# A transformer block on one core: the same instructions in another written-out order of the five engines

## The chip, the core and the metric

The kernel runs on one core of a Trainium2 chip. The metric is the device time of one execution in microseconds (us), and a kernel's time is the median of its runs. The engines are named as in the profile: PE is the matrix engine (PEld its loading of weights), DVE the vector engine, ACT the scalar engine, POOL the GpSimd engine, SP the sync engine, which here only issues DMAs.

## What is computed

A pre-norm block of two parts on 2048 tokens of width 512, in bf16. Part A is linear attention with 32 heads of 16; part B is a gated MLP whose gate mixes the tokens with a 2048x2048 matrix.

```python
h   = x + A(layernorm(x), wqkv, wo)
out = h + B(layernorm(h), w_in, w_sp, b_sp, w_out)

def A(x, wqkv, wo):                 # S = 2048, D = 512, 32 heads
    q, k, v = split(x @ wqkv)
    phi = lambda t: where(t > 0, t + 1, exp(t)) + 1e-6
    kv  = einsum('bhsd,bhse->bhde', phi(k), v)
    den = einsum('bhqd,bhd->bhq', phi(q), sum_s phi(k)) + 1e-6
    o   = einsum('bhqd,bhde->bhqe', phi(q), kv) / den
    return o @ wo

def B(x, w_in, w_sp, b_sp, w_out):  # F = 1792, Fh = 896
    z  = gelu(x @ w_in)
    z1, z2 = z[..., :Fh], layernorm(z[..., Fh:])
    g  = einsum('ts,bsf->btf', w_sp, z2) + b_sp[:, None]
    return (z1 * g) @ w_out
```

## The kernel before

**Stages.** Tokens go in 16 tiles of 128. In the order of the span:

- 0 to 48 us, `k_unit` and `q_unit`: tiles of x are loaded and normalised (`stats` L535, then `rstd` L541 and L543 on POOL or Ln and Exp on ACT, then `norm` L580 on DVE). The first six tiles are transposed on PE (`pe_transposes`, L594, with a copy by ACT), the others by a DMA. Then come k = xn wqkv (L427), phi on ACT and DVE (L606 to L611), and the product of pk with xn over all tokens (L684).
- 48 to 75: v is folded into a matrix m; the denominators are products of pqT with zc (L801), their reciprocals are spread over partitions by DMAs (`spread`, L792), and DVE multiplies pqT by them (L817, "pqT<-pqT,r"). Then for each tile n, PE multiplies pqT by m, DVE adds x and sums the row in one instruction (L829, "h<-psum,x"), and ACT takes the squares ("sh<-h"). POOL turns the two sums into mean and reciprocal deviation: `moments` (L559, L561, L562) and `rpow` (L575) for tiles 0 and 1, `moments_pair` (L567 to L571) for the others. DVE normalises (L580, "hn<-h,st,rs"), and a DMA transposes hn into hnT (L460).
- 70 to 141: B's first matrix, as sums and seven products in place of eight (`hn_sums`, `cell3`, `cell2`). `add_on` (L866) adds a partial result within PSUM on DVE, and PE goes on in the same bank. gelu runs on ACT ("z<-psum", "z1t<-psum"). For z2, even tiles have their squares on ACT ("sq<-z") and `moments` and `rpow` on POOL; the others have bn_stats and bn_aggr on DVE (L943, L944) and L541 and L543 on POOL. `norm` (L580, "z<-z,st,rs") follows on DVE. `t1_sums` and `t_sums` (L863) make sums of z2.
- 104 to 216, overlapping: `mix` multiplies by w_sp, in sums and products again, partly nested twice (`nested`, products of 128x224, with copies within PSUM by ACT and additions by DVE, L1039). `gate` (L999) and `gate_p` (L1007, L1008) form z1*(g + b) on DVE; a DMA on SP transposes it ("zgT<-z1t"). The memory of z1t of some tiles is used again, so that gelu of a later tile waits for such a transpose.
- 143 to the end: `mo_pair` multiplies zgT by w_out (L1158 and L1170 on DVE add h), `mo` (L1138) does the last two tiles, and SP and ACT store.

**What sets the order.** The program first collects 1306 operations with their dependencies (`add`). `schedule` then reads one list of operation numbers from the string ORDER (L16); each engine runs its operations in the order in which they stand in that list. `emit` writes each engine's stream and a semaphore wait for each dependency on another engine or on a DMA that is not already covered. Every engine works through its queue in that order: an instruction that waits holds all that stand behind it on its engine.

```python
ids = np.frombuffer(zlib.decompress(base64.b85decode(ORDER)), np.uint16).tolist()
...
self.seq = [self.ops[i] for i in ids]
self.order = {e: [o for o in self.seq if o.eng == e] for e in self.ENGS}
```

The costs and latencies that the operations carry (`dve_cost`, `act_cost`, `lat=`) give start times in `schedule`; in this program these only sort the waits of one operation.

Of the kernel before, what the change touches and what calls it, by code (L numbers as in the profile page):

```python
# [252 lines left out]
def bass_sequential_preLN__linear_attn_block__mixer_gmlp__prompt_kernel(  # L253
# [155 lines left out]
    def bank(b, n=512, lo=0):  # L409
        return psum[:, b, lo:lo + n]  # L410
# [39 lines left out]
    def dve(fn, reads, writes, n, ps=False, acc=1, **k):  # L450
        return g.add("DVE", fn, reads, writes, cost=dve_cost(n, ps, acc), lat=95, **k)
# [63 lines left out]
    load_x("ACT", 1, 1, 2300)  # L515
    x2 = load_x("SP", 2, 1, 2300)
    load_x("ACT", 3, 1, 2550)
    first_load("SP", wqkv[:, 0:2, D:2 * D], A_wqkv[0:2 * P, D:2 * D], "wka", 4200)
    wk = first_load("ACT", wqkv[:, 2:4, D:2 * D], A_wqkv[2 * P:4 * P, D:2 * D], "wkb", 4400)
    for n, lat, behind in ((4, 4600, None), (6, 3400, x2), (8, 3850, wk), (10, 4000, wk), (12, 4200, wk), (14, 4400, wk)):  # L520
# [12 lines left out]
    def stats(src, k, n):  # L533
        s = st[k][:, n, :]
        dve(lambda v: v.bn_stats(s[:, 0:6], src[:, n, :]), [src[:, n, :]], [s[:, 0:6]], D)  # L535
        return dve(lambda v: v.bn_aggr(s[:, 6:8], s[:, 0:6]), [s[:, 0:6]], [s[:, 6:8]], 14)

    def rstd(s, r, n, w, col, neg, sign=1.0):

# [16 lines left out]
    def moments(s, col, n):  # L556

        mean, ve = s[:, col:col + 1], s[:, col + 1:col + 2]
        pool(lambda p: p.tensor_scalar(s[:, 2:3], s[:, 0:1], s[:, 0:1], -1.0 / (n * n), op0=ALU.mult, op1=ALU.mult), [s[:, 0:1]],  # L559
             [s[:, 2:3]], 240)  # L560
        pool(lambda p: p.tensor_scalar(ve, s[:, 2:3], s[:, 1:2], EPS_LN, op0=ALU.add, op1=ALU.add), [s[:, 1:3]], [ve], 240)  # L561
        pool(lambda p: p.tensor_scalar(mean, s[:, 0:1], 1.0 / n, None, op0=ALU.mult), [s[:, 0:1]], [mean], 190)  # L562

    def moments_pair(i, n):
        s, r = st[1][:, i:i + 2, :], rs[1][:, i:i + 2, 0:1]
# [6 lines left out]
             740)  # L572

    def rpow(ve, r):
        pool(lambda p: p.tensor_tensor(r, ve, expo[:, 0:1], ALU.pow), [ve, expo], [r], 620)  # L575
# [25 lines left out]
    def phi(dst, b, w=2, split=False):  # L601

        e, t = e_t[ecnt[0] % NE][:, 0:w, :], psum[:, b:b + w, :]
        ecnt[0] += 1
        act_exp(e, t, ACT.Exp, w * GW)
        dve(lambda v: v.tensor_scalar(e, e, 1.0, EPS_PHI, op0=ALU.min, op1=ALU.add), [e], [e], w * GW, acc=4)  # L606
        if split:
            act(dst, t, ACT.Identity, w * GW, bias=epst[:, 2:3], extra=[epst[:, 2:3]])
            dve(lambda v: v.tensor_tensor(dst, dst, e, ALU.max), [dst, e], [dst], w * GW, acc=2)
        else:  # L610
            dve(lambda v: v.scalar_tensor_tensor(dst, t, 1.0 + EPS_PHI, e, op0=ALU.add, op1=ALU.max),  # L611
                [t, e], [dst], w * GW, ps=True)

    def warmup(n, ns, behind=None):
        def fn(pe):
# [172 lines left out]
    def spread(tg, c, w):  # L788
        i = tg % 2
        src, dst = rcp[32 * c:32 * (c + 1), i:i + w, :], r16[tg // 2][:, c, i:i + w, :]  # L790
        src_ap = bass.AP(src.tensor, src.offset, [list(src.ap[0]), [0, 4], [1, w * GW]])
        g.add("SP", lambda q: q.dma_start(dst, src_ap), [rcp[:, i:i + w, :]], [dst], cost=700, lat=2200, dma=f"r{tg}{c // 2}").soft.add(win_last.i)  # L792

    for tg in range(NG):
        tok = slice(tg * GW, (tg + 1) * GW)
# [29 lines left out]
    for n in range(NT):  # L825
        b = AB[n % 3]
        matmuls(bank(b), [(pqT[:, c, n * P:(n + 1) * P], m[:, c, :]) for c in range(KD)])
        s = st[1][:, n, :]
        dve(lambda v, n=n, b=b, s=s: v.scalar_tensor_tensor(h[:, n, :], bank(b), 1.0, x[:, n, :], op0=ALU.mult, op1=ALU.add,  # L829
                                                            accum_out=s[:, 0:1]),  # L830
            [bank(b), x[:, n, :]], [h[:, n, :], s[:, 0:1]], D + 70, ps=True)
        act(sh_t[n % 2], h[:, n, :], ACT.Square, D, scale=D ** -0.5, accum=s[:, 1:2])
        if n < HPAIR:
            moments(s, 6, D)
            rpow(s[:, 7:8], rs[1][:, n, 0:1])
            done = [n]
        else:
            done = [n - 1, n] if n % 2 else []
            if done:
                moments_pair(n - 1, D)  # L840
        for i in done:
            hn = hn_t[i % NH]
            norm(HN(i), hn, h[:, i, :], st[1], rs[1], i, 6, D)
            g.last = dma_t(hnT[:, :, i * P:(i + 1) * P], hn, f"ht{i}")
# [8 lines left out]
    def half(b):  # L853
        return bank(b, HW)
# [76 lines left out]
    def z2_done(n, b):  # L931
# [7 lines left out]
        else:  # L939
            gl = act(dst, two(b), ACT.Gelu_apprx_tanh, FH)  # L940
            for k in (0, 1):
                c = slice(k * HW, (k + 1) * HW)
                dve(lambda v, c=c, k=k: v.bn_stats(s[:, 6 * k:6 * k + 6], z2[:, n, c]), [z2[:, n, c]], [s[:, 6 * k:6 * k + 6]], HW)  # L943
            dve(lambda v: v.bn_aggr(s[:, 12:14], s[:, 0:12]), [s[:, 0:12]], [s[:, 12:14]], 14)  # L944
# [23 lines left out]
    SETS = (0, 3)  # L968
    Z1C = {1: (0,), 3: (1,), 5: (4,), 7: (5,)}
    ZLATE = (2, 6, 3, 7)  # L970
    NEST, ONPOOL = (0, 3, 15, 7), ()
    HB = 2
    SQ = range(0, NT - 2, 2)
    w_sums(win2, wq1[1])
# [5 lines left out]
    for j in range(HT):  # L980
# [9 lines left out]
        for q in Z1C.get(j, ()):  # L990
# [3 lines left out]
            for n in (2 * q, 2 * q + 1):  # L994
                z1_tile(n, 6)

    def gate(n, c, b):
# [4 lines left out]
    cnt = [0]  # L1002

    def gate_p(n, c, b, p):
        o, u = z1[n][:, c], u_t[cnt[0] % 2]
# [225 lines left out]
```

## Time and profile before

| | us |
|---|---|
| median of 3 runs | 227.09 (226.91 to 227.54) |
| profiled execution, whole time | 227.38 |
| profiled execution, span | 225.5 |
| PE busy, share of the span | 218.1, 97% |
| DVE busy | 204.9, 91% |
| ACT busy | 138.0, 61% |
| POOL busy | 51.5, 23% |

The span runs from the first to the last instruction of the profiled execution; its whole time is 1.9 us longer. A line of the profile names the line of the kernel, the engine, the operation and `out<-in`; L12 is line 12 of the kernel, and a helper's line stands for all who call it (L427 is every product, L446 every ACT operation). In the timeline a line begins with start and duration in us; in square brackets stands how long the engine was idle before it, and who released it. Neighbouring instructions of one kind are shown as one line, with their number behind the x.

### The profile page before, as it was taken

What the parts mean: (1) busy time and instruction counts of PE and PEld (TensorE: products, weight loads), DVE (VectorE), ACT (ScalarE), POOL (GpSimd) and SP (SyncE); (2) the same over time, 40 slices, a digit from 0 to 9 for tenths busy, and PEclk for the clock granted to TensorE, in tenths of its full rate; (3) what the DMA queues carried; (4) which work ended last, traced back from release to release, by engine and by line L of the source; (5) the groups of instructions that cost most, each with busy time, mean ns of one, the idle gap of its engine ahead of it and who ended that gap; (6) DMA issues with size and microseconds to landing.
All of it is one profiled execution on the core that took longest, in us unless ns stands there. A gap on an engine that the chain in (4) does not pass through costs nothing.

```text
span 225.5 us, 3882 instructions
## 1 busy us (share of the span) xinstructions
PE 218.1 (97%) x1361; PEld 125.6 (56%) x1361; DVE 204.9 (91%) x473; ACT 138.0 (61%) x274; POOL 51.5 (23%) x134
## 2 busy tenths in 40 slices
PE   8899999999999999999999999999999999999995
PEld 7434444453334454544555555767678668885653
DVE  4899855699999999989999999999999999999884
ACT  5686735479969999999675335543235824664111
POOL 2455400000384874597720000000000000000000
PEclk9999999999999999999999999999999999999999
DMA  5736478936553344699990225999061520262474
GB/s 160 241 104 150 75 209 246 241 70 159 125 116 70 70 93 74 132 174 184 217 199 7 41 44 103 182 181 132 0 128 34 97 58 9 65 67 87 85 188 148
DMA packets 73907, 26.87 MB, mean 119 GB/s; under 512 B 63648, under 2 KB 73888, under 8 KB 73888
## 3 DMA queue, kind: packets, MB, share of 16 engines
q1 hardware_dynamic: 73184, 26.03, 54.8%
q10 hardware_dynamic: 704, 0.59, 0.9%
q8 instruction: 11, 0.18, 0.3%
q14 instruction: 8, 0.07, 0.1%
HBM read 6.95 MB, written 2.10 MB: 40 GB/s over the span
## 4 chain that ended last, share of the span: by engine, by line
PE 66%; ACT 13%; DVE 8%; POOL 5%; DMA 4%; issue 2%; SPq 1%; ACTq 0%
PE psum L427 59%; PE psum L684 6%; ACT z L446 3%; DMA x<-in_A_x_dram 3%; DVE h L829 2%; ACT z1t L446 2%; ACT sq L446 2%; POOL rs L575 2%; DMA zgT<-z1t 1%; DVE st L535 1%; ACT psum L446 1%; ACT p5z L446 1%; DVE h L1170 1%; ACT sh L446 1%; ACT ct L446 1%
## 5 line engine op out<-in xcount | busy, mean ns | idle before, releaser
L446 ACT ACTIVATE psum<-psum 128x448 f32<-128x448 f32 (+2 forms) x76 | 31.5, 425 | 36.6 <-PE psum L427 29.7
L427 PE MATMUL psum<-z,wt 128*128 128x448 bf16 (+1 forms) x216 | 41.9, 335 | 0.0
L427 PEld LDWEIGHTS psum<-z,wt 128*128 128x128 bf16 x216 | 21.1, 98 | 14.9
L427 PE MATMUL psum<-win,hnT 128*128 128x448 bf16 x112 | 26.3, 353 | 0.0
L446 ACT ACTIVATE e<-psum 128x1024 bf16<-128x1024 f32 (+1 forms) x18 | 16.7, 928 | 14.1 <-PE psum L427 13.6
L446 ACT ACTIVATE z1t<-psum 128x448 bf16<-128x448 f32 (+1 forms) x24 | 16.2, 678 | 12.7 <-PE psum L427 9.9
L427 PE MATMUL psum<-zt,sa 128*128 128x448 bf16 (+1 forms) x120 | 22.2, 321 | 0.0
L427 PE MATMUL psum<-ws,hs 128*128 128x448 bf16 x72 | 19.0, 353 | 0.0
L446 ACT ACTIVATE p<-psum,b 128x448 f32<-128x448 f32 x22 | 13.5, 633 | 6.2 <-PE psum L427 4.3
L427 PEld LDWEIGHTS psum<-win,hnT 128*128 128x128 bf16 x112 | 10.5, 98 | 10.9 <-ACT z1t L446 0.9
L427 PE MATMUL psum<-xnT,wqkv 128*128 128x512 bf16 x64 | 15.6, 379 | 0.2 <-DVE pqT L611 0.2
L866 DVE TENSOR_TENSOR psum<-psum,p5z 128x448 f32<-128x448 f32 x24 | 15.1, 628 | 0.9 <-PE psum L427 0.4
L427 PE MATMUL psum<-wqkv,xnT 128*128 128x512 bf16 x64 | 15.4, 379 | 0.4 <-DMA wqkv<-in_A_wqkv_dram 0.4
L427 PE MATMUL psum<-m,pqT 128*128 128x512 bf16 x64 | 15.0, 380 | 0.7 <-DVE h L829 0.7
L427 PE MATMUL psum<-wout,zgT 128*128 128x256 bf16 (+1 forms) x77 | 15.2, 302 | 0.2 <-DVE h L1170 0.2
L427 PEld LDWEIGHTS psum<-zt,sa 128*128 128x128 bf16 x120 | 11.7, 98 | 6.5
L684 PE MATMUL psum<-pk,xn 128*128 128x512 bf16 x64 | 15.3, 379 | 0.0
L446 ACT ACTIVATE z<-psum 128x896 bf16<-128x896 f32 x16 | 14.9, 946 | 0.5 <-PE psum L427 0.2
L427 PE MATMUL psum<-nv,nu 128*128 128x224 bf16 x108 | 14.4, 259 | 0.0
L1007 DVE TENSOR_TENSOR u<-psum,p 128x448 bf16<-128x448 f32 x22 | 13.7, 622 | 0.5 <-PE psum L427 0.3
L606 DVE TENSOR_SCALAR e<-e 128x1024 bf16<-128x1024 bf16 (+1 forms) x18 | 7.1, 397 | 7.4 <-ACT e L446 7.2
L559 POOL TENSOR_SCALAR st<-st 128x1 f32<-128x1 f32 x10 | 4.2, 422 | 40.9 <-ACT sh L446 36.5
(147 smaller groups left out, 455.1 us busy)
## 6 DMA issues: line engine op xcount, KB each, us to landing
r<-rcp SPq DMA_DIRECT2D x16, 128.0 KB, 2.6
out_dram<-h SPq DMA_DIRECT2D x15, 128.0 KB, 1.9
win<-in_B_w_in_dram SPq DMA_DIRECT2D x2, 896.0 KB, 6.1
x<-in_A_x_dram SPq DMA_DIRECT2D x6, 256.0 KB, 4.2
wqkv<-in_A_wqkv_dram SPq DMA_DIRECT2D x2, 512.0 KB, 4.2
wout<-in_B_w_out_dram SPq DMA_DIRECT2D x1, 896.0 KB, 6.2
wo<-in_A_wo_dram SPq DMA_DIRECT2D x1, 512.0 KB, 4.9
wt<-in_B_w_sp_dram SPq DMA_TRANSPOSE x32, 4.1
```

Of the source, the lines that this page charges most:

```text
L427: inst = pe.matmul(out_ap, lhsT=a, rhs=b, start=start and i == 0, stop=stop and i == len(pairs) - 1, **kw)
L446: return g.add("ACT", lambda ac: ac.activation(out_ap, in_ap, func, **kw), [in_ap, *extra], [out_ap] + ([accum] if accum is not None else []),
L535: dve(lambda v: v.bn_stats(s[:, 0:6], src[:, n, :]), [src[:, n, :]], [s[:, 0:6]], D)
L559: pool(lambda p: p.tensor_scalar(s[:, 2:3], s[:, 0:1], s[:, 0:1], -1.0 / (n * n), op0=ALU.mult, op1=ALU.mult), [s[:, 0:1]], [s[:, 2:3]], 240)
L575: pool(lambda p: p.tensor_tensor(r, ve, expo[:, 0:1], ALU.pow), [ve, expo], [r], 620)
L606: dve(lambda v: v.tensor_scalar(e, e, 1.0, EPS_PHI, op0=ALU.min, op1=ALU.add), [e], [e], w * GW, acc=4)
L684: inst = pe.matmul(bank(CB[c]), lhsT=xn[:, i, c * P:(c + 1) * P], rhs=pk[:, i, :], start=i == 0, stop=i == NT - 1)
L829: dve(lambda v, n=n, b=b, s=s: v.scalar_tensor_tensor(h[:, n, :], bank(b), 1.0, x[:, n, :], op0=ALU.mult, op1=ALU.add, accum_out=s[:, 0:1] ...
L866: dve(lambda v: v.tensor_tensor(half(b), half(src), p, ALU.add), [half(src), p], [half(b)], HW, ps=True)
L1007: dve(lambda v: v.tensor_tensor(u, half(b), p, ALU.add), [half(b), p], [u], HW, ps=True)
L1170: dve(lambda v, o=o, q=q, add=add: v.tensor_tensor(o, q, add, ALU.add), [q, add], [o], DH2, ps=True)
```

## The change

The five engines get another order: the string ORDER is replaced by one that decodes to another list of the same 1306 numbers. The two programs have the same operations, buffers and dependencies (351 operations on PE, 457 on DVE, 246 on ACT, 130 on POOL, 122 on SP). Besides that, costs that the operations carry are altered, and `gate` gets a second form that no tile uses (GACT is empty).

```diff
-ORDER = "c-jrt)1oB^5Cgz;I%n?Kwr$(CZQHhO ...
+ORDER = "c-jrs1EM7e5Cgz;(r^CQwr$(CZQHhO ...
 ...
     def dve_cost(n, ps, acc=1):
-        return n / acc / 0.96 + 58
+        return n / acc / 0.96 + 68
     def act_cost(n, ps):
-        return n / 1.2 + (49 if ps else 92)
+        return n / 1.2 + (59 if ps else 92)
 ...
-    def dma_t(out_ap, in_ap, name, issue=1310.0, lat=1600.0, **k):
+    def dma_t(out_ap, in_ap, name, issue=1270.0, lat=1300.0, **k):
 ...
-             [s[:, 2:3]], 240)
+             [s[:, 2:3]], 360)
 ...
     def gate(n, c, b):
         o = z1[n][:, c]
-        dve(lambda v: v.scalar_tensor_tensor(o, half(b), b32[:, n:n + 1], o, op0=ALU.add, op1=ALU.mult),
-            [half(b), b32[:, n:n + 1], o], [o], HW, ps=True)
+        if n in GACT:
 ...
```

What moves on each engine, with the times of the profile before to find the place:

| place | before | after |
|---|---|---|
| head, PE | three transposes, a product of k, the fourth transposes | four transposes, then the products |
| head, PE | transposes of tile 4, product L684 of tile 0 | L684 of tile 0, transposes of tile 4, L684 of tile 1 |
| head, ACT | four copies of transposed x, then the first exp | three copies, the exp, the fourth copy |
| 60 to 65, POOL | L559, L561, L562, L575 of tile 1 finish before tile 0's L561 | L561 of tile 0 first, the others alternate, L575 of tile 0 before tile 1's |
| 62 to 70, ACT | the load of the gelu table (L847) at 68.58, behind nine squares | directly behind the last reciprocal's exp (61.54) |
| 64 to 68, DVE | norm of tile 1 before L829 of tiles 8 and 9 | behind them |
| 96 to 103, POOL | L543 of tile 7, moments and L575 of tile 6, L543 of tile 5, moments of tile 8 | L541 and L543 of tile 5 and moments of tile 8 first, then tiles 6 and 7 |
| 96 to 104, ACT | square of tile 8 behind two gelus | ahead of them |
| 99 to 104, DVE | norms of tiles 7, 4, 5, 6 between bn_stats, then L866 | norm of tile 5, four bn_stats of tiles 9 and 11, norm of tile 4, L866, norms of tiles 7 and 6 |
| 109 to 140, SP | transposing loads of wt7 and half of wt15 before all transposes of zgT | wt7 behind zgT of tile 0, half of wt15 behind that of tile 1 |
| 55, SP and ACT | load and copy of b_sp | at about 98, among the loads of w_sp |
| 141 to 216, PE, DVE, ACT | pieces of `mix` and `mo_pair` | the same pieces, dealt out differently, by up to some ten places |
| 165 to 225, SP | transposes of zgT, halves of wt14, stores | the stores and the halves of wt14 in other places between the transposes |

More of the change, by code (lines that the diff above doesn't have):

```diff
@@ L517, in bass_sequential_preLN__linear_attn_block__mixer_gmlp__prompt_kernel @@
     load_x("ACT", 3, 1, 2550)
-    first_load("SP", wqkv[:, 0:2, D:2 * D], A_wqkv[0:2 * P, D:2 * D], "wka", 4200)
-    wk = first_load("ACT", wqkv[:, 2:4, D:2 * D], A_wqkv[2 * P:4 * P, D:2 * D], "wkb", 4400)
-    for n, lat, behind in ((4, 4600, None), (6, 3400, x2), (8, 3850, wk), (10, 4000, wk), (12, 4200, wk), (14, 4400, wk)):
+    first_load("SP", wqkv[:, 0:2, D:2 * D], A_wqkv[0:2 * P, D:2 * D], "wka", 5050)
+    wk = first_load("ACT", wqkv[:, 2:4, D:2 * D], A_wqkv[2 * P:4 * P, D:2 * D], "wkb", 5280)
+    for n, lat, behind in ((4, 5330, None), (6, 4150, x2), (8, 3100, wk), (10, 3280, wk), (12, 4150, wk), (14, 4350, wk)):
         load_x("SP", n, 2, lat, behind)
@@ L535, in stats @@
         dve(lambda v: v.bn_stats(s[:, 0:6], src[:, n, :]), [src[:, n, :]], [s[:, 0:6]], D)
-        return dve(lambda v: v.bn_aggr(s[:, 6:8], s[:, 0:6]), [s[:, 0:6]], [s[:, 6:8]], 14)
+        return dve(lambda v: v.bn_aggr(s[:, 6:8], s[:, 0:6]), [s[:, 0:6]], [s[:, 6:8]], 42)
     def rstd(s, r, n, w, col, neg, sign=1.0):
@@ L559, in moments @@
         pool(lambda p: p.tensor_scalar(s[:, 2:3], s[:, 0:1], s[:, 0:1], -1.0 / (n * n), op0=ALU.mult, op1=ALU.mult), [s[:, 0:1]],
[L560 to L562 removed]
+             [s[:, 2:3]], 360)
+        pool(lambda p: p.tensor_scalar(ve, s[:, 2:3], s[:, 1:2], EPS_LN, op0=ALU.add, op1=ALU.add), [s[:, 1:3]], [ve], 270)
+        pool(lambda p: p.tensor_scalar(mean, s[:, 0:1], 1.0 / n, None, op0=ALU.mult), [s[:, 0:1]], [mean], 560)
     def moments_pair(i, n):
@@ L574, in rpow @@
     def rpow(ve, r):
-        pool(lambda p: p.tensor_tensor(r, ve, expo[:, 0:1], ALU.pow), [ve, expo], [r], 620)
+        pool(lambda p: p.tensor_tensor(r, ve, expo[:, 0:1], ALU.pow), [ve, expo], [r], 680)
     def norm(eng, dst, src, s, r, n, col, w):
@@ L605, in phi @@
         act_exp(e, t, ACT.Exp, w * GW)
-        dve(lambda v: v.tensor_scalar(e, e, 1.0, EPS_PHI, op0=ALU.min, op1=ALU.add), [e], [e], w * GW, acc=4)
+        dve(lambda v: v.tensor_scalar(e, e, 1.0, EPS_PHI, op0=ALU.min, op1=ALU.add), [e], [e], w * GW + 300 * (w - 1), acc=4)
         if split:
@@ L611, in phi @@
             dve(lambda v: v.scalar_tensor_tensor(dst, t, 1.0 + EPS_PHI, e, op0=ALU.add, op1=ALU.max),
-                [t, e], [dst], w * GW, ps=True)
+                [t, e], [dst], w * GW + 40, ps=True)
     def warmup(n, ns, behind=None):
@@ L791, in spread @@
         src_ap = bass.AP(src.tensor, src.offset, [list(src.ap[0]), [0, 4], [1, w * GW]])
-        g.add("SP", lambda q: q.dma_start(dst, src_ap), [rcp[:, i:i + w, :]], [dst], cost=700, lat=2200, dma=f"r{tg}{c // 2}").soft.add(win_last.i)
+        g.add("SP", lambda q: q.dma_start(dst, src_ap), [rcp[:, i:i + w, :]], [dst], cost=640, lat=2150, dma=f"r{tg}{c // 2}").soft.add(win_last.i)
     for tg in range(NG):
@@ L970, in bass_sequential_preLN__linear_attn_block__mixer_gmlp__prompt_kernel @@
     ZLATE = (2, 6, 3, 7)
-    NEST, ONPOOL = (0, 3, 15, 7), ()
+    NEST, ONPOOL, GACT = (0, 3, 15, 7), (), ()
     HB = 2
@@ L995, in bass_sequential_preLN__linear_attn_block__mixer_gmlp__prompt_kernel @@
                 z1_tile(n, 6)
+    cnt = [0]
     def gate(n, c, b):
         o = z1[n][:, c]
-        dve(lambda v: v.scalar_tensor_tensor(o, half(b), b32[:, n:n + 1], o, op0=ALU.add, op1=ALU.mult),
-            [half(b), b32[:, n:n + 1], o], [o], HW, ps=True)
-    cnt = [0]
+        if n in GACT:
+            u = u_t[cnt[0] % 2]
+            cnt[0] += 1
+            act(u, half(b), ACT.Identity, HW, bias=b32[:, n:n + 1], extra=[b32[:, n:n + 1]])
+            dve(lambda v: v.tensor_tensor(o, u, o, ALU.mult), [u, o], [o], HW, acc=2)
+        else:
+            dve(lambda v: v.scalar_tensor_tensor(o, half(b), b32[:, n:n + 1], o, op0=ALU.add, op1=ALU.mult),
+                [half(b), b32[:, n:n + 1], o], [o], HW + 60, ps=True)
     def gate_p(n, c, b, p):
```

6 lines of the change are left out of this document (3 added, 3 removed).

## The prediction

> **What bounds the kernel now.** I read the shares first: PE is busy 97% of the span and DVE 91%, and the granted clock is 1.00 in every row. The same matmuls run in both kernels, so only PE's idle time can be won. Next I read the table by stretches, cut where PE stops (busy us and number of instructions, PE, PEld, DVE, ACT, POOL):
>
> ```profile
> core 0: us, PE busy (x) PEld busy (x) DVE busy (x) ACT busy (x) POOL busy (x), PEclk, DMA share, GB/s
> ...
> 48.00:66.80 18.80, 17.78 (x100) 7.07 (x99) 18.08 (x43) 16.14 (x32) 5.91 (x15) 1.00 0.51 117
> 66.80:103.00 36.20, 36.20 (x187) 17.13 (x185) 34.67 (x88) 35.90 (x73) 23.85 (x55) 1.00 0.54 104
> 103.00:104.20 1.20, 0.70 (x4) 0.31 (x4) 1.20 (x4) 1.12 (x3) 1.04 (x4) 1.00 1.18 247
> 104.20:138.70 34.50, 34.50 (x191) 18.28 (x188) 33.87 (x69) 19.74 (x38) 8.23 (x18) 1.00 0.56 104
> 138.70:141.60 2.90, 2.35 (x17) 1.36 (x17) 2.87 (x7) 1.82 (x6) 0.00 (x0) 1.00 0.82 168
> 141.60:216.00 74.40, 74.40 (x558) 53.83 (x557) 72.42 (x183) 33.02 (x81) 0.00 (x0) 1.00 0.48 87
> ```
>
> PE has no gap in 145 us of it (66.8 to 103, 104.2 to 138.7, 141.6 to 216). What can be won lies at the head, in 48 to 66.8, at 103 and at 139 to 141. DVE is nearly as full, and ACT is full from 66.8 to 103, so an engine that waits in its queue there soon holds PE. The waits view then says on whom PE waited, and for the same release what DVE waited for (us in all, times, longest):
>
> ```profile
> PE psum L427 <- DVE psum L866: 1.1, 3, 0.5
> ...
> PE psum L594 <- DVE xn L580: 0.8, 2, 0.5
> PE psum L427 <- DVE h L829: 0.7, 2, 0.5
> ```
> ```profile
> DVE z L580 <- POOL rs L543: 0.9, 2, 0.4
> ...
> DVE hn L580 <- POOL rs L575: 0.5, 1, 0.5
> ```
>
> So a normalisation at the head of DVE's queue waits for POOL's small steps, and what PE needs stands behind it. The timeline shows both places. At 66:
>
> ```profile
> 63.68 1.09 POOL L575 TENSOR_TENSOR rs<-st,expo 128x1 f32<-128x1 f32 x1
> ...
> 64.80 0.41 DVE L580 TENSOR_SCALAR hn<-h,st,rs 128x512 bf16<-128x512 bf16 x1 [0.48 <-POOL rs L575]
> ...
> 65.13 0.68 DVE L829 SCALAR_TENSOR_TENSOR h<-psum,x 128x512 bf16<-128x512 f32 x1
> ...
> 65.88 1.68 PE L427 MATMUL psum<-m,pqT 128*128 128x512 bf16 x7 [0.46 <-DVE h L829]
> ```
>
> and at 103:
>
> ```profile
> 97.78 1.30 POOL L543 TENSOR_TENSOR rs<-rs,expo 128x1 f32<-128x1 f32 x1
> ...
> 99.11 0.94 DVE L580 TENSOR_SCALAR z<-z,st,rs 128x896 bf16<-128x896 bf16 x2 [0.44 <-POOL rs L543]
> ...
> 100.45 0.54 POOL L543 TENSOR_TENSOR rs<-rs,expo 128x1 f32<-128x1 f32 x1
> ...
> 101.03 0.51 DVE L580 TENSOR_SCALAR z<-z,st,rs 128x896 bf16<-128x896 bf16 x1 [0.44 <-POOL rs L543]
> ...
> 103.00 0.63 DVE L866 TENSOR_TENSOR psum<-psum,p5z 128x448 f32<-128x448 f32 x1
> ...
> 103.68 0.55 PE L427 MATMUL psum<-win,hs 128*128 128x448 bf16 x2 [0.50 <-DVE psum L866]
> ```
>
> Against PE's own pitch (128x448 products start 0.189 apart, 128x512 ones 0.216) the lost time is 0.62 us at 65.88, 0.67 at 103.68, 0.54 at 139.11 and 0.34 at 140.98.
>
> **The change, stage by stage.** Nothing is added or removed; each queue is only permuted, mostly by one to three places. The new costs enter only the order in which one instruction's waits are written: 0.
>
> Head, to 16 us. The fourth transposes (L594), at 8.68 now, go ahead of the first products, into the time before the wqkv load lands (PE starts at 7.82); the product L684 of tile 0 goes ahead of the transposes of tile 4, which now wait for DVE's norm until 12.16. The first exp on ACT goes ahead of the last copy of transposed x. Chained by hand: first product 7.9, its exp done 9.6, the copy after it 10.2, PE's fourth product done 11.35; tile 0's factor comes off DVE at 11.79 as now, and the same work is done at 15.9 to 16.2 where it is done at 16.18 now. Ends -0.3 (gain) and +0.2 (the copy behind the exp comes late); I take -0.15.
>
> 48 to 60. The same stalls (0.2 to 0.4 each, on copies by ACT and L829 of DVE) stand behind the same instructions: 0, within 0.1.
>
> 66. POOL's queue now runs tile 1's moments and L575 before tile 0's. In the new order tile 0's are interleaved and its L575 comes first. Tile 0's steps could start at 60.5, where its square is done on ACT; with six steps ahead of or in it, of 0.22 to 0.82 each by the rows at 59.98 to 63.59, its L575 ends at 63.4 to 64.0, and 64.77 now. DVE's turn for the norm is 64.3, so the wait of 0.48 goes, L829 of tile 6 starts 0.48 earlier, and PE gains 0.48 of its 0.62. The second norm moves behind two L829, by 1.3 us; its transposed tile is needed at 71 and would land at about 69.9, so that is hidden. The gelu table load (L847, 1.28 us, now at 68.58) moves up in ACT's queue to 62.2, where ACT waits 0.36 at 63.75 and 1.37 at 66.46: it costs nothing there and gives ACT 1.3 us of lead for the full stage after it; without that cover it would cost the 1.28 to the squares of tiles 2 and 3, whose norms come at 67.9 and have 0.7 to spare.
>
> 103. POOL's L541 and L543 of tile 5 go ahead of tile 6's and 7's, and the norms of tiles 7 and 6 go behind L866 on DVE; four bn_stats come ahead of it in their place (0.53 pitch each), with the square of tile 8 moved up on ACT so that POOL can take its moments early. DVE's work ahead of L866 is 0.15 shorter and 0.88 of waiting is gone. With the 0.48 from 66, L866 ends at about 102.1, or 102.45 if tile 5's L543 takes the longest of its rows (1.30, where the row at 100.45 took 0.54). PE, itself 0.6 earlier, wants it at 102.4. So 0.67 goes, or 0.55 in the bad case: I take 0.6.
>
> 104 to 141. DVE has no gap there, PE none to 138.7; both are ahead by about the same, and their order is changed by swaps with 0.3 us or more to spare by DVE's pitches. The stalls at 139 and 141 hang on a chain (L999, the transpose of zgT, ACT's z1t, L866) of which every member moves with the lead: they stay, 0 gained. On SP the two transposes of wt7 and the first of wt15 now stand between those of zgT (1.3 us of issue each). zgT of tile 1 is issued at about 130.2 where it is 129.41, and 1.2 earlier with the lead; zgT of tile 8 still finds SP free. Cost 0, at most the 0.5 by which an idle queue's landing (3.27) could grow beside another transpose.
>
> 141.6 to 216. PE loses nothing now, so nothing is to be won, and most of the reordering is here. By adding DVE's start-to-start times in the new order, each sum or addition stays ahead of the product that needs it, by 0.13 us at the closest (L863's last nu at 142.9) and over 0.4 elsewhere. About eight products come closer to the ACT copy that they need (0.71 to 1.04 us of PE work between, for a copy of 0.346 or 0.371 and about 0.28 of handing over, so 0.05 to 0.4 to spare). A miss costs about 0.1 each: +0.1 in all, ends 0 and 0.5.
>
> Tail. The last chain (L1170 at 216.65, L1138) keeps its order: 0.
>
> The sum: -0.15 - 0.48 - 0.6 + 0.1 = -1.13. The profiled execution took 227.38 (225.5 of span and 1.9 around it), which gives 226.25; it stands 0.29 above the median of 227.09, so for a median I forecast **226.0**.
>
> **The rivals.** About 0.3% (0.7 us) is what a measurement of this kernel can tell from none, so I call less than that the same.
>
> A, POOL's steps stay slow and give the gains back. L575 ran 1.09 at 63.68 while DVE multiplied pqT by r (63.63 to 64.32, two operands in SBUF), and L543 ran 1.30 at 97.78 beside a sum of zt (97.58 to 98.67), against 0.54 beside bn_stats. In the new order L543 of tile 5 is beside that sum again, and tile 0's chain beside another multiplication by r. If both are stretched as in these rows, and L561 too (0.78 at 62.50), the norm at 64.3 still waits 0.3, the one before L866 0.35, and L866 meets PE with 0.3 of stall left: the gain is 0.15 + 0.2 + 0.3 - 0.1 = 0.55, or 226.5. [...] Against A: DVE's turn comes late enough that most of a stretched step is covered. 0.17.
>
> B, the waits are not what binds. The swaps all fall in covered places, and what DVE and PE gain at 66 is lost where ACT or a DMA holds them (36.20 us with 35.90 of ACT): no change, 227.1. For it: ACT's stage. Against it: the table load leaves that stage. 0.1.
>
> C, slower: ACT's copies within the nested products (141.6 to 216) come late. They share ACT's queue with reads of 0.54 (128x448) and 0.63 (L446 with bias), and ACT is busy 33.02 of 74.40, 44%. If a copy meets such an instruction it starts up to 0.63 late. At eight places 0.15 each takes back the gain of 1.13; at 0.3 each, and with the same loss to DVE, which has 2 us to spare in the whole stage, it is 2.4 lost: 227.09 - 1.13 + 2.4 = 228.4. For it: the distances did shrink. Against: PE never waits for ACT in this stage now, though several distances are already 0.66 to 0.77. 0.18 for coming out slower by this.
>
> **How the numbers follow.** The forecast gets 0.55. Its own range is 225.3 (the head's -0.3, all of 0.62 and 0.67, and 0.2 off the stall at 139) to 226.4. A (226.5) and B (227.1) stand next to it, C beyond. The range for 8 in 10 leaves out most of C and a little below: 225.2 to 227.9. Faster by over 0.3%: the forecast's 0.55 and a little of A, 0.57. The same: the rest of A, and B, 0.24. Slower: C and 0.01, 0.19.
>
> **What would show it.** Right: no wait of DVE's hn on L575 at 64, none over 0.2 of z on L543 near 99 to 101, PE without a gap at 102 to 103, the stalls at 139 and 141 there but about 1.1 earlier, and the last stretch of 74.4 with at most 0.2 of idle PE. Wrong: PE waits for ACT psum in the nested products (C), L543 or L575 of over 1 us with DVE idle behind it (A), or the stall at 103 gone while the one at 139 has grown by as much (B).

## The result

The changed order takes 228.68 us (median of 6 runs, 228.19 to 229.48), the kernel before 227.22 in the runs beside it: the ratio is 1.0068, with a 95% interval of 1.0045 to 1.0091, so 1.5 us slower. The forecast was 226.0. The profiled execution took 228.32 (226.1 of span and 2.2 around it), 0.94 more than that of before. In the changed file the lines behind 997 stand lower by six or eight: L1007 is the old L999, L1176 the old L1170.

The table by stretches of the changed kernel, with the columns and the cuts of the one shown for the kernel before:

```profile
...
48.00:66.80 18.80, 18.18 (x100) 7.49 (x101) 18.57 (x44) 17.75 (x33) 4.88 (x14) 1.00 0.50 119
...
103.00:104.20 1.20, 1.15 (x7) 0.41 (x5) 1.20 (x3) 1.14 (x3) 1.10 (x2) 1.00 0.95 186
104.20:138.70 34.50, 33.77 (x186) 17.62 (x183) 32.94 (x66) 18.32 (x35) 7.82 (x16) 1.00 0.60 115
138.70:141.60 2.90, 1.70 (x12) 1.08 (x12) 2.50 (x5) 1.92 (x6) 0.00 (x0) 1.00 0.33 73
141.60:216.00 74.40, 74.04 (x550) 53.73 (x557) 72.93 (x184) 33.14 (x82) 0.00 (x0) 1.00 0.54 87
...
```

PE lost 1.02 of 18.80 at 48 to 66.8 before and loses 0.62 at most now; the 0.50 at 103 are 0.05. So the two gains forecast are there. What is new is 0.73 of idle PE in 104 to 138.7, where there was none, and 1.20 in place of 0.55 at 138.7 to 141.6. The page counts 1347 matmuls in place of 1361: records missing from this trace (all 1361 weight loads are there). The 0.36 of idle PE in the last row is mostly theirs, since PE falls no further behind in that stretch (table below, 140 to 215). PE's waits (us in all, times, longest):

```profile
PE psum L427 <- DVE psum L866: 1.8, 2, 1.6
...
```

The wait for L829 of 0.7 is gone, one of 0.5 for a DMA at 21 is new, and a single wait for L866 of 1.6 is longer than the three of before together. Both programs do the same products. So one can take the places where both have done the same set, and compare the times of their weight loads. PE is ahead of the old execution by (us, below zero behind it):

| at (time before) | 17 | 23 | 64 | 68 | 95 | 104.5 | 125 | 134.9 | 140 | 180 | 215 |
|---|---|---|---|---|---|---|---|---|---|---|---|
| changed kernel | 0.47 | -0.08 | 0.02 | 0.49 | 0.59 | 1.19 | 0.94 | 0.56 | -0.66 | -0.50 | -0.66 |

So 0.47 came at 66 and 0.60 at 103, of which 0.25 went by 125; 0.55 were lost at 21, 0.38 at 133 and 1.22 at 138. The reordering of 141 to 216 moved nothing by its end.

At 66 (timeline; start and duration):

```profile
62.71 0.57 POOL L575 TENSOR_TENSOR rs<-st,expo 128x1 f32<-128x1 f32 x1
...
64.32 0.41 DVE L580 TENSOR_SCALAR hn<-h,st,rs 128x512 bf16<-128x512 bf16 x1
64.65 0.68 DVE L829 SCALAR_TENSOR_TENSOR h<-psum,x 128x512 bf16<-128x512 f32 x1
```

L575 of tile 0 ends at 63.28 in place of 64.77, the norm does not wait, and L829 of tile 6 starts at 64.65 in place of 65.13: the 0.48 of the prediction. At 103:

```profile
98.09 0.55 POOL L543 TENSOR_TENSOR rs<-rs,expo 128x1 f32<-128x1 f32 x1
98.67 0.51 DVE L580 TENSOR_SCALAR z<-z,st,rs 128x896 bf16<-128x896 bf16 x1 [0.80 <-POOL rs L543]
...
101.82 0.60 DVE L866 TENSOR_TENSOR psum<-psum,p5z 128x448 f32<-128x448 f32 x1
...
102.50 0.54 PE L427 MATMUL psum<-win,hs 128*128 128x448 bf16 x2
...
103.18 0.62 DVE L866 TENSOR_TENSOR psum<-psum,p5z 128x448 f32<-128x448 f32 x1
...
103.85 0.11 PEld L427 LDWEIGHTS psum<-win,hs 128*128 128x128 bf16 x2 [0.49 <-DVE psum L866]
```

The first L866 is 1.18 earlier. DVE waits longer for L543 (0.80) than before, but with enough slack behind it. The 0.25 that go again are lost right behind it: the two norms that were moved behind this L866 (102.34 to 103.26 on DVE) now stand ahead of the next one, and PE waits for that at 103.86.

The loss is at 133 to 140 (timeline). Before:

```profile
139.11 0.55 PE L427 MATMUL psum<-win,hs 128*128 128x448 bf16 x2 [0.38 <-DVE psum L866]
```

and in the changed kernel:

```profile
133.17 0.98 ACT L446 ACTIVATE z1t<-psum 128x448 bf16<-128x448 f32 x2 [1.68 <-DMA zgT<-z1t]
133.55 1.22 SPq L460 DMA_TRANSPOSE zgT<-z1t  x1
133.77 0.55 PE L427 MATMUL psum<-win,hnT 128*128 128x448 bf16 x2 [0.20 <-ACT z1t L446]
134.81 1.45 SPq L460 DMA_TRANSPOSE wt<-in_B_w_sp_dram  x1
...
138.51 0.54 ACT L446 ACTIVATE z1t<-psum 128x448 bf16<-128x448 f32 x1 [2.62 <-DMA zgT<-z1t]
139.09 0.63 DVE L866 TENSOR_TENSOR psum<-psum,p5z 128x448 f32<-128x448 f32 x1 [1.57 <-ACT z1t L446]
139.78 0.36 PE L427 MATMUL psum<-win,hs 128*128 128x448 bf16 x1 [1.60 <-DVE psum L866]
```

The chain views give the one piece that differs, the transpose of zgT of tile 8, from issue to landing. Before:

```profile
134.50 3.27 DMA zgT<-z1t
```

and in the changed kernel:

```profile
133.55 4.88 DMA zgT<-z1t
```

It is issued 0.95 earlier and lands 0.66 later. Here and below a stall is the time that PE loses against its pitch: 0.54 at 139.11 before, 1.77 in the changed kernel.

### The profile page after: what moved, and what is told of

It reads as the page before. It is cut to its first block, busy times and chain, and to the rows that moved or that the text cites. A ratio compares the mean times of both kernels' runs of the same rounds, so it can differ in the third digit from the quotient of the medians.

```text
span 226.1 us, 3868 instructions
## 1 busy us (share of the span) xinstructions
PE 217.1 (96%) x1347; PEld 125.6 (56%) x1361; DVE 205.3 (91%) x473; ACT 138.1 (61%) x274; POOL 49.1 (22%) x134
## 4 chain that ended last, share of the span: by engine, by line
PE 63%; ACT 15%; DVE 12%; DMA 6%; issue 1%; POOL 1%; SPq 1%; ACTq 0%
PE psum L427 57%; PE psum L684 5%; ACT z L446 4%; DVE h L829 4%; DMA x<-in_A_x_dram 3%; ACT z1t L446 2%; DMA zgT<-z1t 2%; ACT sq L446 2%; DMA xnT<-xn 2%; ACT e L446 2%; DVE pqT L817 1%; ACT p5z L446 1%; ACT psum L446 1%; DVE st L535 1%; DVE psum L866 1%
## 5 line engine op out<-in xcount | busy, mean ns | idle before, releaser
L866 DVE TENSOR_TENSOR psum<-psum,p5z 128x448 f32<-128x448 f32 x24 | 14.9, 623 | 2.0 <-ACT z1t L446 1.6
L684 PE MATMUL psum<-pk,xn 128*128 128x512 bf16 x63 | 15.4, 379 | 0.3 <-DVE pk L611 0.3
L427 PE MATMUL psum<-wqkv,xnT 128*128 128x512 bf16 x62 | 14.9, 379 | 0.6 <-DMA xnT<-xn 0.5
L427 PE MATMUL psum<-xnT,wqkv 128*128 128x512 bf16 x61 | 15.0, 379 | 0.2
L559 POOL TENSOR_SCALAR st<-st 128x1 f32<-128x1 f32 x10 | 3.9, 390 | 45.7 <-ACT sh L446 36.1
L535 DVE BATCH_NORM_STATS2 st<-x 128x6 f32<-128x512 bf16 x15 | 9.8, 675 | 3.9 <-DMA x<-in_A_x_dram 3.9
```

Of the source, the lines that this page charges most:

```text
L427: inst = pe.matmul(out_ap, lhsT=a, rhs=b, start=start and i == 0, stop=stop and i == len(pairs) - 1, **kw)
L684: inst = pe.matmul(bank(CB[c]), lhsT=xn[:, i, c * P:(c + 1) * P], rhs=pk[:, i, :], start=i == 0, stop=i == NT - 1)
L866: dve(lambda v: v.tensor_tensor(half(b), half(src), p, ALU.add), [half(src), p], [half(b)], HW, ps=True)
```

## The experiments

All are compared with the kernel before, run beside them on the same chip; "1.0068" and the like are ratios to it. The runs come from four chips, so two kernels that did not run side by side are compared by their ratios. Edits of ORDER are shown decoded.

**First: SP's queue, or DVE's order?** The change puts transposing loads of w_sp between the transposes of zgT. Three kernels move only these loads, one the head.

`a_sp_undo`, the changed order with SP's queue put back there:

```diff
-SP: zgT0, wt7a, wt7b, zgT1, wt15a, zgT8, wt15b, zgT9
+SP: wt7a, wt7b, wt15a, zgT0, zgT1, zgT8, zgT9, wt15b
```

> The changed order, with only SP's queue put back at one place: the four transposing loads of wt7 and wt15 stand where they stood before (three ahead of the first transpose of zgT, the fourth behind that of zgT of tile 9). Theory SP: the loads of w_sp beside the transposes of zgT lengthened the landing of zgT of tile 8 from 3.27 to 4.88 us and of tile 1 from 2.9 to 3.5, and made the stall at 138 of 1.77 in place of 0.54; with them back, landing 3.3, stall 0.4 to 0.6, no stall at 133, and the time 1.4 to 1.6 below the changed kernel, 227.1 to 227.3. Rival DVE: the order of DVE brings the pieces of z1t of tiles 1 and 8 later, and the landing was one long sample; then the stall at 138 stays over 1 us and the time falls by less than 0.4.

Measured: 1.0032 (1.0013 to 1.0052), 0.8 us below the changed kernel. The wait at 133 is gone, but the transpose of zgT of tile 8, now alone in the queue, still landed in 4.86, and the stall at 137 was 2.14. Neither theory: DVE's pieces were in time (issue at 133.32), and no load stood beside it.

`b_sp_do`, the kernel before with the opposite edit:

```diff
-SP: wt7a, wt7b, wt15a, zgT0, zgT1, zgT8, zgT9, wt15b
+SP: zgT0, wt7a, wt7b, zgT1, wt15a, zgT8, wt15b, zgT9
```

> The kernel before, with only those four transposing loads on SP moved to where the changed order has them. Theory SP: the landing of zgT of tile 8 becomes 4.5 to 5 us, the stall at 139 grows by 1 to 1.6, and the time is 1.0 to 1.6 over the kernel before. Rival DVE: within 0.3 of the kernel before.

Measured: 1.0056 (1.0034 to 1.0078). The transpose of zgT of tile 1 waited for SP until 129.85 (its data were ready at 128.47) and landed 3.52 later, and PE stalled 1.0 at 132.9; that of tile 8 took 4.41. So SP's order costs in the old order too, but the two transposes have to be told apart.

`a_wt15b`, the changed order with the second half of wt15 behind the transpose of tile 9:

```diff
-SP: zgT0, wt7a, wt7b, zgT1, wt15a, zgT8, wt15b, zgT9
+SP: zgT0, wt7a, wt7b, zgT1, wt15a, zgT8, zgT9, wt15b
```

> The changed order, with only the second half of wt15 moved back on SP, behind the transpose of zgT of tile 9; both halves of wt7 and the first of wt15 stay between those of zgT. If the load issued directly behind zgT of tile 8 (1.26 us later) lengthens its landing, landing is 3.3 and the time 1.0 to 1.4 below the changed kernel; if the one issued 2.7 us ahead of it does, landing stays at 4.5 or more and the time is within 0.3 of the changed kernel.

Measured: 1.0041 (1.0021 to 1.0061), landing 4.57. So it is not the load behind it, though the time is 0.6 below the changed kernel, and not within 0.3.

`a_head_undo`, the changed order with the old head:

```diff
-all engines, 0 to 27 us: new order
+all engines, 0 to 27 us: order of before
```

> The changed order, with the head up to 27 us (all five engines) as before. The profile of the changed kernel has PE 0.26 us ahead at 16 and 0.1 to 0.2 behind after a wait of 0.5 for the DMA transpose of xn at 21.5. Theory: the norms and copies on ACT in the new order make that transpose 0.32 later, and the new head loses 0.1 to 0.4 in all: the time falls by 0.1 to 0.4 and PE has no wait at 21.5. Rival: the head gains 0.26 net and its undoing costs as much.

Measured: 1.0040 (1.0026 to 1.0055), below the changed kernel by more than forecast (0.6), with 0.26 in place of 0.65 lost at 21. The stall at 138 was 1.31 in this profile and 1.77 in the changed kernel's, so part of the difference is not the head's.

**What the packets say.** The DMA view of `a_sp_undo` from issue to landing (40 slices of 0.12 us: busy tenths of the 16 engines, then GB/s):

```profile
DMA  0000000000799999900000000000000999017999
GB/s 0 0 0 0 0 0 0 0 0 13 153 364 201 201 182 71 8 0 0 0 0 0 0 0 4 8 8 10 8 10 10 203 293 255 5 21 138 188 219 217
...
q8 instruction: 1, 0.02, 2.1%
```

The transpose's data start 1.1 us after its issue and move for 0.9 us; then there is nearly nothing for 1.7 us (135.4 to 137.1), until they go on. Among them begins one packet of another queue: q8, of the kind "instruction", 16384 bytes. It begins at 134.65 and takes 1.67, to 136.31. The kernel before has such a packet too, from 134.83, but there the data of the transpose began only at 135.6. In the kernel before eleven of these come in the execution, after 92, 228, 347, 466, 614, 720 of its 1361 weight loads and so on, 126 weight loads apart on average; in the changed kernel they come after 94, 227, 347, 466, 612, 730, and in all kernels with this warm-up within some 20 weight loads of the same places. What they are for, and why they come there, is not shown. That this one goes with PE's instructions and not with the clock, and that it is what holds the transpose, was my guess at this point; the next runs test it.

**Second: move the packet alone.** If the packet follows PE's instructions, 14 more of them ahead bring it earlier at this place by an estimated 14 x 0.189 = 2.6 us (0.189 is the measured pitch of 128x448 products). They go into the warm-up, before PE has its data (`warmup` gets the width of a matmul as a further argument):

```diff
-    second = warmup(16, 60, op)
+    second = warmup(30, 60, op, 64)
```

`a_spu_f14`, `a_sp_undo` with these:

> The changed order with SP's four loads of w_sp put back, and 14 more matrix instructions in the second warm-up (30 of 128x64 in place of 16 of 128x128, results unused). Theory FETCH: with the SP loads put back the transpose of zgT of tile 8 still took 4.86 us to land because a packet of 16 KB on queue 8 (kind instruction, 134.65 to 136.3) stood among its packets; queue 8's packets come at the same place of PE's stream (720 to 730 weight loads done), so 14 more matmuls ahead bring this one about 2.5 us earlier, to 132 to 133.5, out of the transfer. Landing 2.9 to 3.3, the stall at 137 of 2.14 becomes 0.4 to 0.6, and the time falls by 1.2 to 1.7 against the same kernel without the 14 (ratio 1.0032 to the kernel before): 226.2 to 226.9. Rival: the landing is long for what the lead brings it beside, whatever the fetch; then landing stays over 4.4 and the time within 0.3.

Measured: 0.9938 (0.9919 to 0.9957), 225.77 us: 2.1 us below `a_sp_undo` by the ratios, more than the 1.2 to 1.7 forecast. The DMA view from issue to landing:

```profile
DMA  0000000000000000399999999999997300000000
...
q1 hardware_dynamic: 928, 0.23, 39.4%
```

No q8 (the packet now comes at 131.53, 3.12 earlier than in `a_sp_undo`), no hole, landing 2.96. The timeline:

```profile
136.38 0.54 ACT L446 ACTIVATE z1t<-psum 128x448 bf16<-128x448 f32 x1 [1.08 <-DMA zgT<-z1t]
136.95 0.63 DVE L866 TENSOR_TENSOR psum<-psum,p5z 128x448 f32<-128x448 f32 x1
137.64 0.55 PE L427 MATMUL psum<-win,hs 128*128 128x448 bf16 x2
```

L866 waits for nothing, and of PE's stall of 2.14 about 0.2 is left.

`b_f14`, the kernel before with the same 14 (the same edit as above):

> Control: the kernel before with the same 14 more matrix instructions in the warm-up. The packet of queue 8 at 134.83 comes 2.5 us earlier. Both theories: landing of zgT of tile 8 between 2.9 and 3.3, the time within 0.4 of the kernel before.

Measured: 0.9967 (0.9949 to 0.9985), 226.34 us; packet at 132.16, 2.67 earlier than in the kernel before, landing 2.95. That is 0.8 faster, outside the 0.4 expected. The kernel before had paid for the packet as well: 0.32 of its stall of 0.54 is gone. Of PE's lead of 0.92 at 215 in this profile, another 0.42 comes at 103, where the stall is 0.25 (see `b103_f14`), and 0.18 is there at 23; these two owe nothing to this packet.

`b_fm7`, the kernel before with fewer:

```diff
-    second = warmup(16, 60, op)
+    second = warmup(9, 60, op, 128)
```

> The kernel before with 7 fewer matrix instructions in the second warm-up (9 in place of 16). Theory FETCH: the packet of queue 8 comes 1.3 us later, at 136.0 to 136.3, among the packets of zgT of tile 8 (135.6 to 137.2); its landing goes from 3.27 to 4.3 or more, the stall at 139 from 0.54 to 1.5 to 2, and the time rises by 0.8 to 1.4 with the order of before untouched. Rival: landing 3.3 and the time within 0.3 of the kernel before.

Measured: 1.0049 (1.0030 to 1.0069), 1.1 us slower, as forecast. Its DMA view:

```profile
DMA  0000000000399999990000000000001999000299
...
q8 instruction: 1, 0.02, 1.4%
```

The packet begins at 135.79, 0.96 later than in the kernel before and inside the data, there is the same hole, landing is 4.54 and the stall 1.82. The old order, made slower by seven unused instructions fewer.

`a_best1`, `a_spu_f14` with the old head (the edit of `a_head_undo`):

> The changed order with three things mended: SP's four loads and the head up to 27 us as before, and 14 more matrix instructions in the warm-up. What is left are the reorderings at 66 and 103 and in 141 to 216. Theory: the 0.5 and 0.6 gained there now reach the end, and 0.1 to 0.3 come from the shorter landing: 1.0 to 1.4 below the kernel before, 225.8 to 226.3. Rival: PE is held again at 133 to 141 by something else, and it is within 0.4 of the kernel before.

Measured: 0.9939 (0.9918 to 0.9960), 225.82 us, the same as with the new head.

In these profiles landing goes with the place of the packet after the issue of the transpose (of zgT of tile 8):

| kernel | issue | packet begins | after issue | landing takes |
|---|---|---|---|---|
| a_spu_f14 | 133.34 | 131.53 | -1.81 | 2.96 |
| b_f14 | 133.89 | 132.16 | -1.73 | 2.95 |
| a_f7 (below) | 133.42 | 133.25 | -0.17 | 2.94 |
| before | 134.50 | 134.83 | 0.33 | 3.27 |
| a_sp_undo | 133.32 | 134.65 | 1.33 | 4.86 |
| b_fm7 | 134.01 | 135.79 | 1.78 | 4.54 |
| b_sp_do | 133.58 | 135.50 | 1.92 | 4.41 |
| a_head_undo | 133.32 | 135.81 | 2.49 | 4.69 |
| a_wt15b | 133.34 | 135.90 | 2.56 | 4.57 |
| changed kernel | 133.55 | 136.25 | 2.70 | 4.88 |

The other transposes of zgT bear this out. There are 16 in each of the 17 profiles, 272 in all. In 203 of them no such packet begins between 0.5 ahead of the issue and the landing, and they land in 2.86 to 3.76. In 42 one begins 1.0 or more behind the issue: 38 of these land in 3.97 to 4.88, and the other four, with the packet 2.36 to 2.80 behind the issue, in 2.9. In the remaining 27 it begins between the two, and they land in 2.94 to 4.50.

**Third: the price of each part, with the packet moved away.** All have the 14 warm-up instructions unless told otherwise; `b_f14` (0.9967, on another chip) is the base.

`a_f14`, the whole changed order (the edit of the warm-up alone):

> The changed order complete, SP's loads of wt7 and wt15 in their new places, with 14 more matrix instructions in the warm-up. It gives the price of SP's new order with the packet of queue 8 out of the way. Theory: the packet costs 1.2 to 1.7 here too, and SP's new order about 0.4 to 1.0 (zgT of tile 1 lands in 3.5 to 3.7 in place of 2.9, and PE waits 0.4 to 0.6 for z1t at 133): 226.3 to 226.9, ratio to the kernel before 0.996 to 0.999. Rival: SP's order is free without the packet: 225.6 to 226.0, as with the loads put back.

Measured: 1.0010 (0.9990 to 1.0030), outside both ranges. The transpose of tile 8 landed in 3.01, but the packet (131.92) now fell into that of tile 1, which landed in 4.78:

```profile
134.61 0.36 PE L427 MATMUL psum<-win,hnT 128*128 128x448 bf16 x1 [1.51 <-ACT z1t L446]
```

In `a_spu_f14` the packet comes at nearly the same time, but with SP's old queue that transpose's data had moved by then (landed 132.07).

`a_f7`, the whole changed order with half as many:

```diff
-    second = warmup(16, 60, op)
+    second = warmup(23, 60, op, 64)
```

> The changed order complete, with 7 more matrix instructions in the warm-up (23 of 128x64) in place of 14. With 14, the packet of queue 8 (131.92) fell into the transpose of zgT of tile 1, which SP's new order makes later; with 7 it should come at about 133.2, between the two transposes. Theory: zgT of tile 1 lands in 3.5 to 3.7 and zgT of tile 8 in 3.0; PE waits 0.3 to 0.6 for z1t at 133 and 0.3 to 0.6 at 138: the price of SP's order alone is 0.3 to 0.7, and the time is 226.1 to 226.7, ratio 0.995 to 0.998. Rival: SP's order costs 1.2 or more by itself: 227.2 or more, as with 14.

Measured: 0.9989 (0.9973 to 1.0006), median 226.90, between the two ranges. In the profiled execution (226.03) the packet stood at 133.25, between the two transposes; they landed in 3.32 and 2.94, PE waited 0.2 at 133 and had no stall at 138. Two of the twelve runs are at 226.0 and ten at 226.7 to 227.3. By the profiled executions SP's new queue costs 226.03 - 225.59 = 0.44 where no packet hits (that of `a_spu_f14` took 225.59); these are two single executions on two chips, so 0.44 is an estimate. By the medians it is 1.1; what the ten met was not profiled.

The next five take the old order with a stretch of the new, all engines alike:

```diff
-order of before
+order of before, in it the new order from 58.5 to 71.6 us (b66_f14), 43.5 to 71.6 (b44_66_f14),
+90 to 105.6 (b103_f14), 0 to 27.6 (bhead_f14), 0 to 43.5 (bhead43_f14)
```

`b66_f14`:

> The kernel before with the 14 warm-up instructions (ratio 0.9967 by itself) and the new order of all five engines from 58.5 to 71.6 alone. Theory: the wait of DVE for L575 goes, PE's stall of 0.62 at 65.9 becomes 0.2 or less, and 0.4 to 0.5 of it reaches the end: ratio 0.994 to 0.996. Rival: the lead is lost by 141: ratio 0.996 to 0.998.

Measured: 0.9953 (0.9926 to 0.9979), not to be told from the base; PE's lead at 95 is 0.17 as in the base (0.19). New stalls of 0.28 and 0.34 at 63.0 and 64.1 took the place of the 0.62.

`b44_66_f14`:

> The kernel before with the 14 warm-up instructions (median 226.34 by itself) and the new order of all engines from 43.5 to 71.6. The new order from 58.5 on alone brought PE nothing (stalls of 0.28 at 63.0 and 0.34 at 64.1 took the place of the 0.62). Theory: the stall at 66 needs the swaps from 48 to 58 too (the spreads of r and the products of pqT with r come in another order), and with them PE is 0.4 to 0.6 ahead at 95 and at the end: 225.7 to 226.0. Rival: the gain comes from elsewhere: no lead at 95, 226.2 to 226.5.

Measured: 1.0041 (1.0020 to 1.0061), a miss by the time, but for a reason of its own: at the seam with the old order, at 74.6, PE stalled 1.95. Before the seam it went as forecast: no stall at 62.5 to 66, and a lead of 0.44 at 48 and 1.01 at 68, a gain of 0.57.

`b103_f14`:

> The same with the new order from 90 to 105.6 alone. The stall at 103 was 0.67 in the profile of the kernel before but 0.25 in three other profiles of its order, and 0.22 in all of the new order. Theory: this part is worth 0.0 to 0.3 on most runs: ratio 0.9955 to 0.9968. Rival, the prediction's term: 0.6: ratio 0.994.

Measured: 0.9961 (0.9943 to 0.9980), as the theory had it. PE gains 0.60 up to 104.5, loses 0.24 of it again by 125, and the base gains as much: with the old order there the stall is 0.25 in five profiles and 0.67 in three, that of before among these. The two cases differ on POOL ahead of the second L543: L562 and L575 take 0.50 and 0.73 in the three (99.16 and 99.74 in the kernel before), 0.23 and 0.62 in the five. Why they take one or the other is not shown.

`bhead_f14`:

> The same with the new head alone, up to 27 us. Theory: PE gains 0.2 to 0.3 by 17 us and loses it at 21 to the DMA transpose of xn, which comes 0.3 later: 0.0 to 0.3 slower, ratio 0.9967 to 0.998. Rival, the prediction's term: 0.15 faster.

Measured: 1.0027 (1.0001 to 1.0053), outside the forecast. Its stall of 0.8 at 38.2 is the seam's (a DMA transpose of xn stands late), so this one says nothing of the head after 27.

`bhead43_f14`:

> The kernel before with the 14 warm-up instructions and the whole new order up to 43.5 us. The cut at 27 us left a DMA transpose of xn at its late place and a stall of 0.8 at 38.2 that neither whole order has. Theory: without that the new head is worth -0.1 to +0.2, and the median is 226.1 to 226.6. Rival: the head really costs 0.5 or more: 226.9 or more.

Measured: 0.9980 (0.9963 to 0.9996), median 226.82, between the two ranges. PE is 0.29 ahead at 17 and 0.33 behind at 23, after a stall of 0.7 on the DMA transpose of xn. The ratio cannot be told from the base. Over all profiles PE at 23 is ahead of the kernel before by 0.17 on average with the old head (nine, from -0.14 to 0.47) and by 0.12 with the new (eight, from -0.33 to 0.39): the new head gains nothing.

## Why the prediction was wrong

- **Head, forecast -0.15:** wrong in its end. At 16 PE is 0.47 ahead, 0.21 of it since 9, so 0.26 was gained, the end of my own range; but I followed the chain only to there. ACT took a norm ahead of two copies and waited 0.34 for POOL; the DMA transposes of xn behind it are issued at 17.65 in place of 17.33, and PE waits for one at 21:

```profile
17.65 5.50 SPq L460 DMA_TRANSPOSE xnT<-xn  x3
...
21.54 1.25 PE L427 MATMUL psum<-wqkv,xnT 128*128 128x512 bf16 x5 [0.49 <-DMA xnT<-xn]
```

With the old head PE waits there too when it comes early (0.33 in `b_fm7`).

- **66, forecast -0.48:** right, 0.47. But the POOL order alone does not give it (`b66_f14`); the swaps between 44 and 58, costed at nothing, belong to it (`b44_66_f14`).
- **103, forecast -0.6:** 0.60 came in this profile, and 0.25 of it went again at 103.86, where PE waits for the next L866 behind the moved norms; the prediction followed DVE only to the first. The 0.67 that I took from one profile is 0.25 in five others of the same order, so against these this part is worth about nothing (`b103_f14`). The term was sized on a long sample.
- **139 and 141, "of which every member moves with the lead: they stay", and SP "Cost 0, at most the 0.5":** the step that failed. The landing of the transpose was carried over as 3.27 to whatever time it is issued. In the changed kernel it was issued 0.95 earlier, but the 16 KB packet on queue 8 began 1.42 later (136.25 in place of 134.83), 2.70 after the issue in place of 0.33, and so among the data. Landing took 4.88 and not 3.27, and the stall of 0.54 became 1.77. In `a_sp_undo` the packet came at 134.65, much as before, and there the earlier issue (133.32) alone brought the data to it. The packet comes after 720 weight loads before, 725 in `a_sp_undo` and 730 in the changed kernel; why it moves by these few is not shown. Move the packet away (`a_sp_undo` to `a_spu_f14`) and the ratio falls by 0.0094, 2.1 us; in the profiles 1.9 of it come at 138. The bound of 0.5 on landing named no row. In the profile of before, transposes of zgT beside another transpose and with no such packet in them landed in 2.88 to 3.22, and there was a longer one: that of tile 12, with the packet in it, took 4.75. SP's loads, the one risk that I saw, cost about 0.4 where nothing hits them (an estimate from two executions, 1.1 by the medians of `a_f7`), and more where they bring the packet into the transpose of tile 1 (`a_f14`).
- **141 to 216, forecast +0.1, and rival C with 0.18:** nothing was lost there. C's mechanism did not occur; that its 228.4 lies near the 228.68 measured is luck.
- **Rival A:** L543 of tile 5 took 0.55, not 1.30; DVE was idle beside it, waiting for it. That wait of 0.80 was covered.
- **Rival B** came nearest: the stall at 139 grew by more than what had been gained at 103. It had a chance of 0.1, and its price ended at no change: that the lead itself could make the next transfer worse was not among the cases.

With the collision and SP's queue mended the order is worth 225.77 against 226.34 (`a_spu_f14` against `b_f14`, side by side on one chip), about 0.6 us, half of the forecast sum. By the profiles this is the part at 66: PE in `a_spu_f14` is 0.14 ahead of the kernel before at 64 and 0.71 at 68, in `b_f14` 0.18 and 0.19, and at 215 the two are still 0.53 apart (1.45 and 0.92).

## To carry to other kernels

Here the next DMA on the chain decided what an early lead was worth: PE was 1.19 ahead at 104.5 and 0.66 behind at 140, after a landing of 4.88 in place of 3.27. So look the landing up packet by packet, with the other queues that move at that time. Where a transfer on the critical chain lands late without a neighbour in its own queue, look for a packet of the kind "instruction" among its data, and try to shift it by a few unused instructions early in PE's stream: here 14 of them brought it 2.67 to 4.33 earlier (134.83 to 132.16 in the kernel before, 136.25 to 131.92 in the changed one), where the estimate was 2.6. Then look what it meets at its new place: in `a_f14` it met the transpose of tile 1, which landed in 4.78. And size a stall on several profiles of the same order before it is written down as a gain.

## What the hardware showed

- With one packet of 16 KB on queue 8 (0.9 to 1.7 us) that began 1.33 to 2.70 after its issue, the DMA transpose of zgT of tile 8 landed in 4.41 to 4.88 (six kernels); with the packet ahead of the issue it landed in 2.94 to 2.96 (three of the table). In `a_wt15b` nearly all data had moved by 135.9, when the packet began, and the last two packets (4 bytes each) came at 136.8, when it had ended. In `a_sp_undo` the transpose does not go on when the packet ends (136.31): up to 137.1 only 29 packets of 256 bytes begin, one at a time, and 22 others that began between 135.01 and 135.33 all end between 137.12 and 137.16, after 1.8 to 2.1. In `b_fm7` it is the same (20 packets end at 137.55 to 137.59, where the large one ended at 136.79). Why the transpose does not go on at once, and why these end together, is not shown: the trace does not name the DMA engine of a packet.
- The transpose of zgT of tile 1 landed in 2.9 with SP's old queue (2.91 in the kernel before) and in 3.3 to 3.8 with loads of w_sp directly ahead of it (3.48 in the changed kernel), where no such packet met it. Other tiles meet the packet too, where nobody waits for them: that of tile 12 in the kernel before took 4.75 (issue 199.00, packet 201.66).
- Seven unused matmuls fewer made the kernel before 1.1 us slower, 14 more made it 0.8 us faster. The fastest version found is the changed order with SP's old queue and the 14: 225.77 us, 0.9938 (0.9919 to 0.9957) of the kernel before.
